# Routed experts on one core: the third tile of rows joins the first weight product, and the last output product moves behind the branches' join

## The chip, the cores and the metric

The kernel runs on one core of a Trainium2 chip. The metric is the device time of one execution in microseconds (us), less being better. Three runs of the kernel before took 781.63, 782.46 and 782.55 us; the median is 782.46.

## The reference

Three layers follow each other: windowed attention with 32 global tokens, a gated channel mixer, and a mixture of eight experts. Only the last one is touched:

```python
logits = einsum('bsd,de->bse', x, w_gate)            # x: 4 x 544 x 512, 8 experts
local_gate = sigmoid(einsum('bsd,de->bse', x, w_local))
for b, s:                                            # 2176 tokens in all
    e = argmax(logits[b, s]) if s == 0 or local_gate[b, s] < 0.5 else prev_e
    h = maximum(x[b, s] @ w1[e], 0)                  # 512 -> 1024
    out[b, s] = softmax(logits[b, s])[e] * (h @ w2[e])   # 1024 -> 512
    prev_e = e
```

So each token goes to one expert. With the inputs of the reference (seed 0) experts 0 to 7 get 242, 127, 267, 483, 495, 321, 218 and 23 tokens: 2, 1, 3, 4, 4, 3, 2 and 1 tiles of 128 rows.

## The kernel before

Everything is computed in fp32 pieces: a value is held as a high part (h) and a rest (l), and each product is three matmuls, `mm3` (lines 21, 23 and 24: high times high, high times rest, rest times high). Experts are numbered from 0 here, as in the code.

The first stage (to about 532 us) does the attention, the mixer and the routing, and already computes expert 0's first tile. The second stage, `Experts.run`, goes through the experts one after the other in an order written by hand. For an expert e:

- `gather` (line 862) fetches its rows from `y` in DRAM by index, one indirect DMA of 128 rows (256 KB) for each tile, issued on POOL; `prep` (lines 869 to 872) transposes half of the features of two tiles (four transposes, one group), and ACT and DVE split them into xh and xl.
- `full` computes two tiles at once. The first product ph = w1 x (96 matmuls with 256 moving columns, weights stationary) is split by ACT (line 883) and DVE (line 884) into hh, hl; then `output` makes two products po = h w2, each of 24 matmuls with 512 moving columns.
- `tail` computes one tile: 24 matmuls of 512 columns with the rows stationary (pht), a relu by ACT into hs (line 912), 8 transposes back (`turn`, lines 898 to 901), and 24 matmuls of 512 columns for po.
- DVE scales po (line 927) and POOL scatters it to the output (line 931).
- The next expert's weights come in eight loads of 512 KB (line 769, SP). `split` (lines 778 and 781) makes h on ACT and l on DVE or POOL. `W` is the list of these splits and `X` the list of the preps of the next expert's rows; `full` and `tail` issue them at fixed places between the matmuls. Five load buffers rotate, so a load is issued when a split has freed its buffer.
- The path is chosen at run time from the number of tiles c: `first` compares c>=2 (line 945), then c==1 (949); `more` compares for the third and the fourth tile (938, 939). Every engine runs these branches. A path that is not taken is jumped over.

```python
with tc.If(c>=2) as two:
    s.full(i,e,0,list(W),[*own,*X])
    s.more(i2,e,1,c)
```

In this stage PE takes the instructions in the order of the code; only when a semaphore or a branch holds them does it stand still.

Of the kernel before, what the change touches and what calls it, by code (L numbers as in the profile page):

```python
# [30 lines left out]
LN=8 ; PL=8  # L31
# [4 lines left out]
NR=4; NP=4  # L36
FX=(3,5,6,7); FW=(2,4,6); NW=(2,3); NST=2
LAT=0.2; DLAT=2.1; SLACK=dict(P=0.15,A=0,D=0,G=0)
# [292 lines left out]
class Mix:  # L331
# [17 lines left out]
    def consts(s,const):  # L349
# [20 lines left out]

        s.up=t([P,E],"up"); nc.gpsimd.memset(s.up,float(P-1)); nc.gpsimd.memset(s.up[:,0:1],-1.0)
        s.last=t([1,1],"last"); nc.vector.memset(s.last,0.0)
# [319 lines left out]
    def finish(s,ps):  # L692

        nc=s.nc; t=s.const
        s.ci=t([P,E],"cint",I32); s.cm=t([P,1],"cmax",I32); cf=t([P,E],"cf")
        nc.vector.tensor_tensor(out=s.ci,in0=ps,in1=s.up,op=ALU.add)
        nc.vector.tensor_scalar(out=s.ci,in0=s.ci,scalar1=7,scalar2=None,op0=ALU.logical_shift_right)
        nc.vector.tensor_copy(cf,s.ci)

        ends=cf[:,0:E:E-1]; nc.vector.tensor_scalar(out=ends,in0=ends,scalar1=3.0,scalar2=None,op0=ALU.add)  # L700
        nc.vector.tensor_reduce(out=s.cm,in_=cf,axis=X,op=ALU.max)
# [49 lines left out]
class Experts:  # L751

    def __init__(s,tc,ident,w1,w2,y,out,slots):
        s.tc=tc; s.nc=tc.nc; s.ident=ident; s.w=(w1,w2); s.y=y; s.out=out
        s.w2done=False; s.slots=slots; s.loaded=0; s.staged=[]; s.K=2

        s.o=[1]+[0]*(E-1); s.m=[1]+[NCH]*(E-2)+[1]
    def slot(s,e,which): return s.slots[((2,0),(1,3))[e%2][which]]
# [89 lines left out]
    def alloc(s):  # L848
        w=s.work

        new=[s.xwork.tile([P,1024],F32,name=f"sw{i}",bufs=1) for i in range(NST)]
        s.x=[[s.xwork.tile([P,4,256],F32R,name=f"x{q}{i}",bufs=1) for q in "hl"] for i in range(3)]
        s.h=[w.tile([P,8,256],F32R,name=f"h{q}",bufs=1) for q in "hl"]
        s.st+=new; s.free+=new
    def row(s,e,k):

        return (k+(e>0))%s.K
# [5 lines left out]
    def prep(s,i,e,k,hf):  # L863

        nc=s.nc; xh,xl=s.x[i]; n=min(2,s.m[e]-2*k); N=n*P
# [7 lines left out]
    def full(s,i,e,k,W,X):  # L873

        nc=s.nc; N=256; w1h,w1l=s.views(e,0); xh,xl=s.x[i]; hh,hl=s.h
        def go(L,n=1):
            for _ in range(n):
                if L: L.pop(0)()
        for f in range(8):
            ph=s.ps.tile([P,512],F32,tag="ph",name="ph",bufs=4)[:,:N]  # L880
            fs=slice(f*P,(f+1)*P)
            for d in range(4): mm3(nc,ph,w1h[:,d,fs],w1l[:,d,fs],xh[:,d],xl[:,d],d==0,d==3)
            nc.scalar.activation(hh[:,f],ph,AF.Relu)  # L883
            nc.vector.scalar_tensor_tensor(out=hl[:,f],in0=ph,scalar=0.0,in1=hh[:,f].bitcast(F32),op0=ALU.max,op1=ALU.subtract)  # L884
            if f in FX: go(X)
            if f in FW: go(W)
        for j in range(2):
            s.output(e,2*k+j,slice(j*P,(j+1)*P),lambda: go(W,NW[j]))
        go(W,8); go(X,8)
    def tail(s,i,e,k,W,X,o=None):  # L890
# [12 lines left out]
        go(W,TW[4])  # L903
        for b in range(2):
            ph=s.ps.tile([P,512],F32,tag="ph",name="pht",bufs=4)
            bs=slice(b*512,(b+1)*512)
            for d in range(4):
                if b and d==2:
                    turn(0,hs[0]); go(W,TW[1])
                mm3(nc,ph,xh[:,d,:P],xl[:,d,:P],w1h[:,d,bs],w1l[:,d,bs],d==0,d==3)  # L910
            hs.append(s.work.tile([P,512],F32,tag="hs",name="hs",bufs=1))
            nc.scalar.activation(hs[b],ph,AF.Relu)
            if b==0: go(W,TW[0])
        def within(f):
            if f==TW[2]: turn(1,hs[1])
            if f in (0,3): go(X)
            if f in TW[3]: go(W)
        s.output(e,2*k,slice(0,P),lambda: (go(X,8),go(W,8)),within,o)
    def output(s,e,c,js,between,within=None,held=None):
        nc=s.nc; w2h,w2l=s.views(e,1); hh,hl=s.h; ch=e*NCH+s.o[e]+c  # L920
        po=s.ps.tile([P,512],F32,tag="po",name="po",bufs=2)
        for f in range(8):
            mm3(nc,po,hh[:,f,js],hl[:,f,js],w2h[:,f],w2l[:,f],f==0,f==7)
            if within: within(f)
        between()
        o=s.work.tile([P,512],F32,tag="osb",name="osb",bufs=2) if held is None else held
        nc.vector.tensor_scalar(out=o,in0=po,scalar1=s.pcol[:,ch:ch+1],scalar2=None,op0=ALU.mult)  # L927
        if held is None: s.scatter(e,c,o)
    def scatter(s,e,c,o):
        ch=e*NCH+s.o[e]+c  # L930
        s.nc.gpsimd.indirect_dma_start(out=s.out,out_offset=IndirectOffsetOnAxis(ap=s.idx[:,ch:ch+1],axis=0),in_=o,in_offset=None,bounds_check=T-1,oob_is_err=False)  # L931
    def more(s,i,e,k,c,d=0):

        tc=s.tc
        if 2*k+2>s.m[e]:
            with tc.If(c>=2*k+1+d): s.tail(i,e,k,[],[])
            return
        with tc.If(c>=2*k+1+d):
            with tc.If(c>=2*k+2+d) as two: s.full(i,e,k,[],[])
            with two.Else(): s.tail(i,e,k,[],[])  # L940
    def first(s,i,i2,e,c,W,own,X):

        tc=s.tc; keep=s.loaded,list(s.staged),list(s.free)
        def again(): s.loaded,s.staged,s.free=keep[0],list(keep[1]),list(keep[2])
        with tc.If(c>=2) as two:
            s.full(i,e,0,list(W),[*own,*X])
            s.more(i2,e,1,c)
        with two.Else():
            with tc.If(c==1) as one: again(); s.tail(i,e,0,list(W),list(X))
            with one.Else():  # L950
                again()
                for g in (*W,*X): g()
    def run(s):
        tc=s.tc; K=s.K

        at=lambda e,k: (e%2,2)[k%2]
        s.gather(0,0)
        _,cs=s.nc.values_load_multi_w_load_instructions(s.counts[0:1,0:E],min_val=0,max_val=NCH); cmax=s.nc.values_load(s.cmax[0:1,0:1],min_val=0,max_val=NCH+3)
        s.cs=cs
# [4 lines left out]
        s.fetch()  # L964
        def own(e): return [lambda hf=hf: s.prep(at(e,1),e,1,hf) for hf in range(2)]
        def others(e):
            if e+1>=E: return []
            def last():
                s.prep(at(e+1,0),e+1,0,1)
                if e+2<E: s.gather(e+2,0)  # L970
            def then():
                if e+2<E: s.gather(e+1,1)
                s.prep(at(e+1,0),e+1,0,0)
            return [then,last]

        s.tail(at(0,0),0,0,[s.whole]*min(8,16-LN),others(0))
        for e in range(1,E-1):
            s.first(at(e,0),at(e,1),e,cs[e],[s.whole]*8,own(e),others(e))
        def weights(e):
            for q in range(8): list(s.split(*s.part(e,q,s.st[q%len(s.st)])))  # L980
        def window(e,k,d):
            i=(0,2)[k%2]
            s.gather(e,k); s.prep(i,e,k,0); s.prep(i,e,k,1)
            s.more(i,e,k,cs[e],d)
        def rest(e,o,load=True):

            d=o-(e==0); keep=s.o[e],s.m[e]
            s.o[e]=o; s.m[e]=NCH-o
            with tc.If(cs[e]>=d+1):
                if load: weights(e)  # L990
                for k in range((s.m[e]+1)//2):
                    with tc.If(cs[e]>=2*k+1+d): window(e,k,d)
            s.o[e],s.m[e]=keep

        s.ol=s.xs[0][:,0]
        def end(): s.tail(at(E-1,0),E-1,0,[],[],s.ol)
        with tc.If(cmax<2*K+1) as usual: end()
        with usual.Else():
            rest(E-1,1,False)
            for e in range(E-1): rest(e,2*K if e else 2)  # L1000
            weights(E-1)
            end()
        s.scatter(E-1,0,s.ol)

# [51 lines left out]
```

## Time and profile before

| | us |
|---|---|
| median of three runs | 782.46 (781.63 to 782.55) |
| the profiled execution, its time | 779.67 |
| its span on the core | 777.9 |
| PE busy in the span | 734.8 |
| stage of the experts in the trace | about 532 to 777.9 |

The profile is one execution. Its span is what the trace covers, and its time is 1.8 us longer. A busy share is an average over both stages; for this change only the second counts. [...] "q" behind an engine's name is its sequencer, which reads branches and fills the engine's queue ahead of execution.

### The profile page before, as it was taken

The numbers are of one execution on the slowest core, as the hardware profiler recorded it, in microseconds if no ns is written. First come the engines' busy times: TensorE is split into PE (matmuls) and PEld (weight loads), VectorE is DVE, ScalarE is ACT, GpSimd is POOL, SyncE is SP. The second block draws the span as 40 slices with busy tenths as digits, with TensorE's granted clock in tenths as the row PEclk, the third lists the DMA queues.
The fourth block names the chain that finished last, engine by engine and source line by source line (L and its number), as shares of the span: only waits on it lengthen the run. The fifth ranks groups of instructions, "written<-read, shape, count | busy, mean of one in ns | idle before, by whom it ended". The sixth has DMA issues, their size and how long they took to land.

```text
span 777.9 us, 14122 instructions
## 1 busy us (share of the span) xinstructions
PE 734.8 (94%) x4782; PEld 621.2 (80%) x4782; DVE 510.5 (66%) x1483; ACT 396.3 (51%) x985; POOL 348.1 (45%) x473
## 2 busy tenths in 40 slices
PE   6889897999999999999999899998799999999996
PEld 3656686888888888888888789776698999989884
DVE  6699978878587694796664865666764643617271
ACT  4788665665374673655653524234662622416151
POOL 6567866742546335545443442013664331614231
PEclk9998798999999999999999899999999999999999
DMA  6584223111211211212000500135886341705320
GB/s 151 146 233 135 78 72 115 45 39 34 66 30 40 63 28 37 66 34 75 20 5 28 190 18 11 55 109 190 302 268 216 127 173 52 256 31 178 127 99 17
DMA packets 93478, 77.04 MB, mean 99 GB/s; under 512 B 70462, under 2 KB 74558, under 8 KB 93378
## 3 DMA queue, kind: packets, MB, share of 16 engines
q1 hardware_dynamic: 89618, 64.27, 27.5%
q0 software_dynamic: 3760, 11.54, 4.3%
q8 instruction: 50, 0.82, 0.4%
q14 instruction: 50, 0.41, 0.2%
HBM read 66.87 MB, written 9.70 MB: 98 GB/s over the span
## 4 chain that ended last, share of the span: by engine, by line
PE 68%; DMA 11%; DVE 7%; issue 7%; ACT 3%; SPq 2%; POOL 1%; POOLq 0%; another core or an unknown queue 0%; ACTq 0%; DVEq 0%
DMA out_dram<-osb,idx 8%; PE av L236 5%; PE psk L21 4%; PE psk L23 4%; PE psv L21 4%; PE psv L23 4%; PE psk L24 4%; PE psv L24 4%; PE ptp L228 3%; PE psr L21 2%; PE po L24 2%; PE po L21 2%; PE psr L24 2%; PE po L23 2%; PE psr L23 2%
## 5 line engine op out<-in xcount | busy, mean ns | idle before, releaser
L222 POOL TENSOR_SCALAR pl<-pl,mx 128x192 f32<-128x192 f32 (+1 forms) x128 | 62.7, 502 | 86.1 <-DVE mx L219 40.6
L21 PE MATMUL psk<-xs,slot0h 128*128 128x256 f32 x256 | 75.1, 299 | 0.8 <-ACT xs L446 0.8
L216 ACT ACTIVATE pl<-pl,mx 128x224 f32<-128x224 f32 (+1 forms) x128 | 58.8, 462 | 32.5 <-DVE mx L213 28.3
L23 PE MATMUL psk<-xs,slot0h 128*128 128x256 f32 x256 | 74.3, 291 | 0.0
L24 PE MATMUL psk<-xs,slot0l 128*128 128x256 f32 x256 | 74.0, 290 | 0.0
L448 POOL TENSOR_TENSOR xs<-xm,xs 128x512 fp32r<-128x512 f32 (+1 forms) x36 | 46.3, 1296 | 40.7 <-ACT xs L446 40.7
L883 ACT ACTIVATE hh<-ph 128x256 fp32r<-128x256 f32 x56 | 21.5, 383 | 84.3 <-PE ph L24 82.5
L441 POOL TENSOR_SCALAR xm<-xT,mut 128x256 f32<-128x256 f32 (+7 forms) x96 | 43.4, 467 | 37.7 <-DVE xT L292 17.9
L862 POOL DMA_INDIRECT xs<-y,idx x26 | 33.0, 1271 | 57.5 <-PE pt L869 33.1
L931 POOL DMA_INDIRECT out_dram<-osb,idx x18 | 22.5, 1252 | 77.2 <-DVE osb L927 59.6
L21 PE MATMUL psv<-slot1h,kh 128*128 128x512 f32 x136 | 55.3, 406 | 0.0
L23 PE MATMUL psv<-slot1l,kh 128*128 128x512 f32 x136 | 54.3, 400 | 0.0
L24 PE MATMUL psv<-slot1h,kl 128*128 128x512 f32 x136 | 54.2, 398 | 0.0
L21 PEld LDWEIGHTS psk<-xs,slot0h 128*128 128x128 f32 x256 | 49.4, 196 | 1.8 <-ACT xs L446 0.9
L23 PEld LDWEIGHTS psk<-xs,slot0h 128*128 128x128 f32 x256 | 49.5, 193 | 1.2
L24 PEld LDWEIGHTS psk<-xs,slot0l 128*128 128x128 f32 x256 | 49.6, 194 | 0.6
L228 PE MATMUL ptp<-ident,pl 128*128 128x128 f32 x256 | 43.5, 290 | 4.6 <-DVE kw L119 1.3
L884 DVE SCALAR_TENSOR_TENSOR hl<-ph,hh 128x256 fp32r<-128x256 f32 x56 | 23.7, 423 | 35.3 <-ACT hh L883 34.9
L236 PE MATMUL av<-ph,v 128*128 128x256 f32 x192 | 44.7, 294 | 2.2 <-DVE xT L292 1.8
L444 DVE SCALAR_TENSOR_TENSOR xm<-xT,mut,xm 128x256 f32<-128x256 f32 (+7 forms) x96 | 42.2, 474 | 3.1 <-POOL xm L441 3.0
L119 DVE TENSOR_TENSOR plo<-ptp,ph 128x512 fp32r<-128x512 f32 x48 | 32.7, 685 | 14.9 <-ACT ph L117 14.6
L228 PEld LDWEIGHTS ptp<-ident,pl 128*128 128x128 f32 x256 | 30.4, 147 | 11.3 <-POOL pl L222 1.9
(732 smaller groups left out, 2456.0 us busy)
## 6 DMA issues: line engine op xcount, KB each, us to landing
st<-in_moe_w_dram SPq DMA_DIRECT2D x42, 512.0 KB
sw<-in_moe_w_dram SPq DMA_DIRECT2D x22, 512.0 KB
y<-r SPq DMA_DIRECT2D x17, 256.0 KB
qn<-in_q_l_dram SPq DMA_DIRECT2D x32, 128.0 KB
kn<-in_k_l_dram SPq DMA_DIRECT2D x32, 128.0 KB
earlyh<-in_moe_w_k_dram SPq DMA_DIRECT2D x8, 512.0 KB
raw<-in_moe_w_v_dram SPq DMA_DIRECT2D x8, 512.0 KB
vn<-in_v_l_dram SPq DMA_DIRECT2D x24, 96.0 KB
```

The lines of the kernel that those rows point to most:

```text
L21: i=nc.tensor.matmul(out,wh,xh,start=first,stop=False)
L23: nc.tensor.matmul(out,wh,xl,start=False,stop=False)
L24: return nc.tensor.matmul(out,wl,xh,start=False,stop=last)
L119: nc.vector.tensor_sub(out[1],x,out[0].bitcast(F32))
L216: nc.scalar.activation(p[:,h,ks],p[:,h,ks],AF.Exp,bias=mx[:,h:h+1],scale=-1.0,accum_out=mx[:,4+h:5+h])
L222: nc.gpsimd.tensor_scalar(out=p[:,h,ks],in0=p[:,h,ks],scalar1=mx[:,6+h:7+h],scalar2=0.0,op0=ALU.mult,op1=ALU.add)
L228: nc.tensor.transpose(pt[:,c,h],p[:,h,c*96:c*96+P],s.ident)
L236: nc.tensor.matmul(o,s.v(u,x,i,c),P_[y][:,c],start=c==m==0,stop=c==1 and m==len(parts)-1)
L441: nc.gpsimd.tensor_scalar(out=x[:,u,o:o+k],in0=s.xT[b][:,c,q:q+k],scalar1=m[:,1,c:c+1],scalar2=0.0,op0=ALU.mult,op1=ALU.add)
L444: nc.vector.scalar_tensor_tensor(out=x[:,u,o:o+k],in0=s.xT[b][:,c,1+q:1+q+k],scalar=m[:,0,c:c+1],in1=x[:,u,o:o+k],op0=ALU.mult,op1=ALU.add)
L448: nc.gpsimd.tensor_sub(xl[:,cs,:n],x[:,:,:n],xh[:,cs,:n].bitcast(F32))
L862: s.nc.gpsimd.indirect_dma_start(out=s.xs[i][:,j,:],out_offset=None,in_=s.y,in_offset=IndirectOffsetOnAxis(ap=s.idx[:,ch:ch+1],axis=0))
```

## The change

The counts that steer the branches are now in units of 32 rows (`up`, `finish`; `tiles(n)=4*n-3` is the first unit of tile n). What else changes:

- Expert 1 is computed as one tile without a branch (`one`), as experts 0 and 7 are; rows above it go to the part for rare cases at the end (`rest`).
- Experts 2 to 6 go through `expert`. A third tile of up to 96 rows is not computed by itself any more: `joined(N)` runs the first product once over N = 288, 320 or 352 rows, then a product for the third tile with 32, 64 or 96 rows stationary (`out_`), then the second tile's product. Which N is chosen stands in a row of comparisons, c>=5, 9, 10, 11, 12, each nested in the one before. From 12 units on `big` runs two tiles and then the third and fourth as before.
- The first tile's output product (for `big` the third's) stands behind the join of all paths (`s.product(0,...)` at the end of `expert`), with the scaling and scatter of bank 1 ahead of it. Which rows it belongs to is copied by POOL into `at` and `by` at the head of each path.
- The third tile's rows are gathered as before and transposed in the expert before (`third`, one group of four transposes, `prep1`); the fourth tile's in `big` alone (`own`).
- Five weight splits stand on each path and three behind the join. x is held for 512 rows in two tiles, h for 352; hs shares the buffers of osb; the descriptor scratch of the indirect DMAs is 4096 bytes instead of 8192.

```diff
-FX=(3,5,6,7); FW=(2,4,6); NW=(2,3); NST=2
+FX=(3,5,7); WJ=(288,320,352); MW=352; FW=(2,4,6); NW=(2,3); NST=2
+def tiles(n): return 4*n-3
-        s.o=[1]+[0]*(E-1); s.m=[1]+[NCH]*(E-2)+[1]
+        s.o=[1]+[0]*(E-1); s.m=[1,1]+[NCH]*(E-3)+[1]
...
+    def wide(s,i,e,N,W=(),X=()):
+        nc=s.nc; W=list(W); X=list(X); w1h,w1l=s.views(e,0); xh,xl=s.rows(i,N); hh,hl=[t[:,:,:N] for t in s.h]
         for f in range(8):
             ph=s.ps.tile([P,512],F32,tag="ph",name="ph",bufs=4)[:,:N]
...
+    def product(s,b,e,js,within={}):
+        w2h,w2l=s.views(e,1); hh,hl=s.h; n=js.stop-js.start
         for f in range(8):
+            mm3(s.nc,s.bank[b][:n],hh[:,f,js],hl[:,f,js],w2h[:,f],w2l[:,f],f==0,f==7)
+            for g in within.get(f,()): g()
+    def place(s,b,pc,idx,n=P,o=None):
+        held=o is not None
+        if not held: o=s.work.tile([P,512],F32,tag="osb",name="osb",bufs=2)[:n]
+        s.nc.vector.tensor_scalar(out=o,in0=s.bank[b][:n],scalar1=pc[:n],scalar2=None,op0=ALU.mult)
+        if not held: s.scatter(o,idx[:n])
...
+    def one(s,i,e,b,W,X,o=None):
+        W=list(W); last=s.tall(i,e,[W.pop(0) for _ in range(min(5,len(W)))])
+        g=dict((f,[]) for f in range(8)); g[TW[2]].append(last)
+        for f,x in zip((0,3,4),X): g[f].insert(0,x)
+        for f,w in zip(TW[3],W): g[f].append(w)
+        s.product(b,e,slice(0,P),g); s.place(b,*s.cols(e,0),o=o)
...
-    def first(s,i,i2,e,c,W,own,X):
+    def expert(s,i,i2,e,c,rows,own,X,third):
+        tc=s.tc; keep=s.loaded,list(s.staged),list(s.free); W=[s.whole]*5
+        def begin(k=0,early=True):
+            s.loaded,s.staged,s.free=keep[0],list(keep[1]),list(keep[2])
+            ch=e*NCH+s.o[e]+2*k
+            s.nc.gpsimd.tensor_copy(s.at,s.idx[:,ch:ch+2]); s.nc.gpsimd.tensor_copy(s.by,s.pcol[:,ch:ch+2])
+            if early: rows()
+        def second(W): s.product(1,e,slice(P,2*P),dict(zip((0,2),([w] for w in W))))
+        def big():
+            begin(1,False)
+            s.wide(i,e,256,W[:3],[own,lambda: (rows(),X[0]()),X[1]])
+            s.out_(0,e,0,slice(0,P),{2:W[:1]}); s.out_(1,e,1,slice(P,2*P),{2:W[:1]})
+            with tc.If(c>=tiles(4)) as four:
+                s.wide(i2,e,256); second([])
+            with four.Else(): s.tall(i2,e,[],[])
+        def joined(N):
+            begin()
+            s.wide(i,e,N,W[:3],X)
+            if N>256: s.out_(0,e,2,slice(256,N))
+            second(W[:2])
...
+        def chain(k):
+            if k==len(L): big(); return
+            with tc.If(c>=tiles(3)+k+1) as up: chain(k+1)
+            with up.Else(): joined(L[k])
+        with tc.If(c>=tiles(2)) as two:
+            with tc.If(c>=tiles(3)) as up: chain(0)
+            with up.Else(): joined(256)
+        with two.Else():
+            with tc.If(c>=1) as some: single()
+            with some.Else(): none()
+        s.place(1,s.by[:,1:2],s.at[:,1:2])
+        s.product(0,e,slice(0,P),{1:[third],2:[s.whole],4:[s.whole],6:[s.whole]})
+        s.place(0,s.by[:,0:1],s.at[:,0:1])
...
-        s.tail(at(0,0),0,0,[s.whole]*min(8,16-LN),others(0))
-        for e in range(1,E-1):
-            s.first(at(e,0),at(e,1),e,cs[e],[s.whole]*8,own(e),others(e))
+        for e in range(2):
+            rows(e); s.one(at(e,0),e,e,[s.whole]*min(8,16-LN if e==0 else 8),[*others(e),lambda: third(e)])
+        for e in range(2,E-1):
+            s.expert(at(e,0),at(e,1),e,cs[e],lambda: rows(e),lambda: own(e),others(e),lambda: third(e))
...
-    nc=_bacc.Bacc("TRN2",target_bir_lowering=False,num_devices=1,dynamic_dma_scratch_size=8192)
+    nc=_bacc.Bacc("TRN2",target_bir_lowering=False,num_devices=1,dynamic_dma_scratch_size=4096)
```

`tall` is `tail` up to its second `turn`; `wide` is the first half of `full`. Three places of PE's order show the moves.

The end of expert 0 and the start of expert 1 on PE, before (slot1 holds expert 1's w1; what follows L945 is the two-tile path, which expert 1 jumps over):

```order
L21 MATMUL po<-slot0h,hh 128x512
L23 MATMUL po<-slot0l,hh 128x512
L24 MATMUL po<-slot0h,hl 128x512
L945 COMPARE_AND_BRANCH
L21 MATMUL ph<-xh_7284,slot1h 128x256
```

and of the change:

```order
L23 MATMUL po_7291<-slot0l,hh 128x512
L24 MATMUL po_7291<-slot0h,hl 128x512
L21 MATMUL po_7291<-slot0h,hh 128x512
L23 MATMUL po_7291<-slot0l,hh 128x512
L24 MATMUL po_7291<-slot0h,hl 128x512
L21 MATMUL pht<-slot1h,xh_7285 128x512
```

The branch is gone, and expert 1's single tile follows directly.

The third tile of expert 2 on PE, before (the second tile's last matmuls, the jump at the end of the two-tile path of lines 938 and 939, the start of the tile by itself):

```order
L23 MATMUL po<-slot3l,hh 128x512
L24 MATMUL po<-slot3h,hl 128x512
L939 UNCONDITIONAL_BRANCH
L21 MATMUL pht<-slot1h,xh_7286 128x512
L23 MATMUL pht<-slot1l,xh_7286 128x512
```

and of the change, on the path for 288 rows (the end of the first product, the start of the third tile's product):

```order
L23 MATMUL ph<-xl_7284,slot2h 128x288
L24 MATMUL ph<-xh_7283,slot2l 128x288
L21 MATMUL ph<-xh_7283,slot2h 128x288
L23 MATMUL ph<-xl_7284,slot2h 128x288
L24 MATMUL ph<-xh_7283,slot2l 128x288
L21 MATMUL po_7291<-slot0h,hh 32x512 [waits Activation_49]
L23 MATMUL po_7291<-slot0l,hh 32x512
L24 MATMUL po_7291<-slot0h,hl 32x512
```

The 24 pht matmuls and the 8 transposes of the third tile are gone; the first product is 32 columns wider, and 24 matmuls with 32 rows stationary follow it.

The join of expert 2's paths on PE in the change (the preps of the empty path, its jump, then the first tile's product and the transposes of expert 3's third tile):

```order
L873 MATMUL pt<-ident,xs_5855 128x128 [waits DVE_49,PE_49]
L873 MATMUL pt<-ident,xs_5855 128x128 x3
L996 UNCONDITIONAL_BRANCH
L21 MATMUL po_7291<-slot0h,hh 128x512 [waits DVE_49,Activation_49]
L23 MATMUL po_7291<-slot0l,hh 128x512
L24 MATMUL po_7291<-slot0h,hl 128x512
L21 MATMUL po_7291<-slot0h,hh 128x512
L23 MATMUL po_7291<-slot0l,hh 128x512
L24 MATMUL po_7291<-slot0h,hl 128x512
```

Before, nothing but the next expert stood behind the join; now 24 matmuls do, whose first one waits for DVE and ACT to have reached the join.

## Rows read from the trace of the kernel before

**Rows 1.** The page: busy us, share of the span and instructions of each engine.
```profile
PE 734.8 (94%) x4782; PEld 621.2 (80%) x4782; DVE 510.5 (66%) x1483; ACT 396.3 (51%) x985; POOL 348.1 (45%) x473
```

**Rows 2.** Stretches of experts 0 to 3, 5, 6: length, busy (matmuls), clock, DMA share, GB/s.
```profile
533.39:548.74 15.35, 13.92 (x64) 1.00 0.87 296
548.74:567.64 18.90, 14.66 (x65) 0.91 0.86 300
567.64:604.07 36.43, 36.40 (x218) 1.00 0.68 232
604.07:650.93 46.86, 46.84 (x306) 1.00 0.38 131
697.71:733.99 36.28, 36.26 (x218) 1.00 0.49 160
733.99:758.90 24.91, 23.91 (x156) 1.00 0.24 83
```

**Rows 3.** Who waited for whom, PE, 530 to 778: total, times, longest.
```profile
PE pht L21 <- DVEq L938: 1.0, 1, 1.0
```

**Rows 4.** Stretches of PE: a 256-wide pass, two 512-wide products, two single tiles.
```profile
628.50:640.01 11.51, 11.51 (x97) 1.00 0.45 175
640.01:650.93 10.92, 10.92 (x50) 1.00 0.07 26
591.84:604.07 12.23, 12.23 (x59) 1.00 0.43 160
721.98:733.99 12.01, 12.01 (x59) 1.00 0.35 134
```

**Rows 5.** The chain in order of time, expert 2: four transposes of one group.
```profile
573.62 0.44 PE pt L869 x4
```

**Rows 6.** Branches on PE's sequencer by line: ns min/median/max, start of the first and last.
```profile
L945 PEldq COMPARE_BRANCH  x1: 7044/7044/7044, 545.7 to 545.7; - x1
L939 PEldq COMPARE_BRANCH  x1: 3896/3896/3896, 587.9 to 587.9; - x1
L939 PEldq COMPARE_BRANCH  x1: 318/318/318, 718.0 to 718.0; - x1
L938 PEldq COMPARE_BRANCH  x1: 3343/3343/3343, 753.7 to 753.7; - x1
```

**Rows 7.** PE in order of time, behind the branches at 545.7 and 587.9: start, length, idle before.
```profile
552.98 0.49 PE L21 MATMUL pht<-slot1h,xh 128*128 128x512 f32 x1 [4.24 <-issue]
591.59 0.39 PE L24 MATMUL po<-slot0h,hl 128*128 128x512 f32 x1
591.84 0.51 PE L21 MATMUL pht<-slot2h,xh 128*128 128x512 f32 x1
```

**Rows 8.** ACT in order of time, expert 1.
```profile
554.90 1.06 ACT L778 ACTIVATE slot2h<-st 128x1024 fp32r<-128x1024 f32 x1 [2.62 <-DMA st<-in_moe_w_dram]
557.68 0.60 ACT L912 ACTIVATE hs<-pht 128x512 f32<-128x512 f32 x1 [1.72 <-PE pht L24]
558.81 0.60 PE L898 MATMUL pht<-ident,hs 128*128 128x128 f32 x4
```

**Rows 9.** Stretches of PE around expert 1: length, busy, clock, DMA share, GB/s.
```profile
545.00:550.00 5.00, 3.74 (x19) 1.00 0.78 254
550.00:555.00 5.00, 2.02 (x6) 0.84 0.96 357
560.00:565.00 5.00, 5.00 (x30) 1.00 0.63 211
553.40:556.70 3.30, 3.30 (x10) 0.50 1.04 377
```

**Rows 10.** PE in order of time, first stage, and the granted clock behind it.
```profile
129.00 0.50 PE L207 MATMUL s__1598<-kw,qT 64*128 64x192 f32 x1 [3.14 <-ACT pg L265]
130.00:133.00 3.00, 3.00 (x8) 0.50 0.00 0
```

**Rows 11.** DMA issues, 545 to 553: count, median us to landing.
```profile
xs<-y,idx POOLq DMA_INDIRECT x4, 8.2
```

More of the change, by code (lines that the diff above doesn't have):

```diff
@@ L872, in prep, with prep1, go @@
         nc.vector.tensor_sub(xl[:,sl,:N],pt[:,:,:N],xh[:,sl,:N].bitcast(F32))
[L873 to L878, printed above, removed]
+    def prep1(s,i,e,k,j):
+        nc=s.nc; js=slice(j*P,(j+1)*P); xh,xl=[t[:,:,js] for t in s.rows(i)]
+        pt=s.ps.tile([P,4,P],F32,tag="pt",name="pt1",bufs=2)
+        for d in range(4): nc.tensor.transpose(pt[:,d],s.xs[s.row(e,k)][:,j,d*P:(d+1)*P],s.ident)
+        nc.scalar.activation(xh,pt,AF.Copy)
+        nc.vector.tensor_sub(xl,pt,xh.bitcast(F32))
+    def go(s,L,n=1):
+        for _ in range(n):
+            if L: L.pop(0)()
+    def wide(s,i,e,N,W=(),X=()):
+        nc=s.nc; W=list(W); X=list(X); w1h,w1l=s.views(e,0); xh,xl=s.rows(i,N); hh,hl=[t[:,:,:N] for t in s.h]
         for f in range(8):
@@ L932, in more, with out_ @@
+    def out_(s,b,e,c,js=slice(0,P),within={}):
+        s.product(b,e,js,within); s.place(b,*s.cols(e,c),n=js.stop-js.start)
+    def one(s,i,e,b,W,X,o=None):
[4 more added lines that the diff above has]
+        s.product(b,e,slice(0,P),g); s.place(b,*s.cols(e,0),o=o)
     def more(s,i,e,k,c,d=0):
@@ L934, in more, with single @@
         tc=s.tc
+        def single():
+            s.tall(i,e,[],[]); s.out_(0,e,2*k)
         if 2*k+2>s.m[e]:
-            with tc.If(c>=2*k+1+d): s.tail(i,e,k,[],[])
+            with tc.If(c>=tiles(2*k+1+d)): single()
             return
-        with tc.If(c>=2*k+1+d):
-            with tc.If(c>=2*k+2+d) as two: s.full(i,e,k,[],[])
-            with two.Else(): s.tail(i,e,k,[],[])
-    def first(s,i,i2,e,c,W,own,X):
[L943 to L947, printed above, removed]
-        with two.Else():
[L949 to L952, printed above, removed]
+        with tc.If(c>=tiles(2*k+1+d)):
+            with tc.If(c>=tiles(2*k+2+d)) as two:
+                s.wide(i,e,256)
+                for j in range(2): s.out_(j,e,2*k+j,slice(j*P,(j+1)*P))
+            with two.Else(): single()
@@ L964, in run, with own, rows, then @@
         s.fetch()
-        def own(e): return [lambda hf=hf: s.prep(at(e,1),e,1,hf) for hf in range(2)]
+        def own(e): s.prep1(at(e,1),e,1,1)
+        def rows(e):
+            if s.m[e+1]>2: s.gather(e+1,1)
         def others(e):
-            if e+1>=E: return []
+            def then(): s.prep(at(e+1,0),e+1,0,0)
             def last():
@@ L988, in rest, with end @@
             s.o[e]=o; s.m[e]=NCH-o
-            with tc.If(cs[e]>=d+1):
+            with tc.If(cs[e]>=tiles(d+1)):
                 if load: weights(e)
                 for k in range((s.m[e]+1)//2):
-                    with tc.If(cs[e]>=2*k+1+d): window(e,k,d)
+                    with tc.If(cs[e]>=tiles(2*k+1+d)): window(e,k,d)
             s.o[e],s.m[e]=keep
         s.ol=s.xs[0][:,0]
-        def end(): s.tail(at(E-1,0),E-1,0,[],[],s.ol)
-        with tc.If(cmax<2*K+1) as usual: end()
+        def end(): s.one(at(E-1,0),E-1,1,[],[],s.ol)
+        with tc.If(cmax<8*K+1) as usual: end()
         with usual.Else():
             rest(E-1,1,False)
-            for e in range(E-1): rest(e,2*K if e else 2)
+            for e in range(E-1): rest(e,(2,1)[e] if e<2 else 2*K)
             weights(E-1)
             end()
-        s.scatter(E-1,0,s.ol)
+        s.scatter(s.ol,s.cols(E-1,0)[1])
 def program(tc,ins,out):
```

82 lines of the change are left out of this document (38 added, 44 removed).

## The prediction

> **What bounds the kernel now.** I read the page first: PE is busy for 94% of the span, the other engines far less [rows 1]. That is an average, so I cut the second stage into its experts [rows 2]. Experts 2, 3, 5 and 6 keep PE busy to within 0.04 us of the whole stretch, except for 1.0 us at the end of expert 6. Expert 1 holds PE for only 14.66 of its 18.90 us, with DMA 86% busy, and expert 0 for 13.92 of 15.35. So from expert 2 on what counts is how long PE's own instructions take, and in experts 0 and 1 what PE waits for. The list of waits names the 1.0 us: expert 7's first matmul waits for DVE's sequencer at the join of line 938 [rows 3]. PE in order of time shows the largest hole, 4.24 us ahead of expert 1, with "issue" as its releaser: no data was late [rows 7]. The row of the branch explains it. PE's sequencer took 7.04 us for the branch of line 945, which began at 545.7 while queued matmuls still ran [rows 6]. Behind the hole the granted clock was 0.50 [rows 9].
>
> **The third tile (experts 2 and 5).** Now it costs a tail of 12.23 us in expert 2 and of 12.01 us in expert 5 [rows 4]. Instead the 96 matmuls of the first product get 32 columns more for expert 2 (267 rows, 9 units, N=288) and 96 more for expert 5 (321 rows, 11 units, N=352), and 24 matmuls of 512 columns are added. A 256-column matmul takes 11.51/96 = 0.120 us and a 512-column one 10.92/48 = 0.2275 us [rows 4], so a column costs 0.00042 us. Widening is 96x32x0.00042 = 1.3 us and 96x96x0.00042 = 3.9 us; the 24 matmuls are 5.5 us (their moving side is the same 512 columns). Balance: -12.2+1.3+5.5 = **-5.5** and -12.0+3.9+5.5 = **-2.7**, together -8.2 us. The trace has no width between 256 and 512. The bounds are a widening that is free (-5.2 us more) and one that costs as much as 512 columns at once (96x0.1076 = 10.3 us for each expert, in place of 1.3 and 3.9). I take the straight line, since 288 lies next to the 256 row and the two rows nearly double with the columns. ACT and DVE work on wider tiles, but they are busy for only 51% and 66% of the span [rows 1], with four ph buffers between.
>
> **Transposes.** A group of four costs 0.44 us [rows 5]. Expert 2 and expert 5 lose one group each, expert 6 two, expert 1 gains one (expert 2's third tile): **-1.3 us**. Experts 3 and 4 have the same four groups and the same products: 0.
>
> **The join ahead of expert 7.** DVE's scaling of expert 6's last product and its branch now run beside 24 matmuls, and expert 7's rows and buffers are long ready: **-1.0 us** [rows 3]. If this cover went, the 1.0 us would be back.
>
> **Expert 1 without a branch.** An undisturbed tile takes 12.01 us [rows 4]; with the two groups that prepare expert 2 it is 12.9. Expert 1 takes 18.90, so 6.0 us are at stake: the 4.24 us hole and some 1.8 us of half clock behind it. But the next stall is near. ACT runs three weight splits ahead of the first relu, and the third waits for its load until 554.90; the relu itself ran at 557.68, when the late matmuls were done, and the transposes on PE at 558.81 [rows 8]. With PE on time ACT is the bound: 554.90+1.06+0.60 lets the transposes start at 556.6, 2.2 us earlier. Three gathers of 256 KB that expert 0 issues for expert 1's further tiles are gone from this stretch, where DMA moves some 300 GB/s [rows 2], 0.79 MB or 2.6 us of its time; the gathers for expert 2 come behind expert 0's scatter instead. Half of that as earlier landing gives 1.3 us. PE then stands still for some 2 us, and the clock may fall again: it was at 0.50 behind holes of 4.24 and of 3.14 us [rows 7, 9, 10]. A quarter of 1.8 us, -0.5. Estimate **-3.0 us**, bounds -0.5 and -6.0. Expert 0's own small savings end in the same wait and count nothing. Expert 2's third rows are now gathered only in expert 1 and needed some 8 us later; gathers landed a median of 8.2 us after issue here [rows 11]. I put **+0.3** for a wait there, bounds 0 and 3.
>
> **New jumps.** A comparison itself is cheap, and five in a row are read while PE's queue is full. A jump is dear when its target must be fetched: lines 939 and 938 took 3.90 and 3.34 us on PE's sequencer, though one at line 939 with the same distance (144 matmuls) took 0.32 [rows 6]. Such a jump is hidden as long as queued matmuls last. The one of 587.9 ended just in time, the next matmul follows at 591.84 without idle time [rows 7]; the one of 753.7 ended ahead of the matmuls at 757.9. So about 4 us are covered behind a dense run of 512-column products, but only 3 us at the end of a single tile: line 945 began at 545.7 and the matmuls ended at 548.7.
>
> The change makes seven long jumps. At the entry expert 2 skips `big` and two wider paths (about 610 matmuls), expert 5 `big` (310), expert 6 `big` and three paths (760). At the join experts 2, 3, 4 and 5 skip 180, 660, 660 and 480 matmuls. Entries of 5 and 6 and all joins lie behind 24 to 48 such products, cover 4 us against 3.3 to 3.9: I put 0.2 us for each, 1.2 us. Expert 2's entry lies behind expert 1's single tile, cover 3 us; DMA was 63% busy there [rows 9], like the 68% of expert 2 [rows 2] where a jump took 3.90 us: 0.9, and 0.5 for contention. Sum **+2.6 us**. Bounds: 0, and for expert 2's entry 7.04-3.0 = 4 us and half clock behind it. [...]
>
> **Rest.** DVE, ACT and POOL jump too, some 1 us or more behind PE; ph buffers cover four feature blocks of 1.5 us each on the entry, 24 matmuls on the join. POOL's two small copies and the earlier gathers delay only rows that are used at the expert's end. The smaller descriptor scratch can hold a gather back by at most what one takes to land, 8.2 us [rows 11]; except in expert 1 (counted) 20 us cover it. All of this: 0.
>
> **Sum.** -8.2-1.3-1.0-3.0+0.3+2.6 = **-10.6 us** on the profiled execution's 779.67 us, so 769.1. The median of the runs is 2.8 us above that execution; I keep this distance: 782.46-10.6 = **771.9 us**.
>
> **Rivals.**
> - *Contended entry* (15%). Expert 2's entry fetches while weights and gathers fill the DMA queues, as line 945 did at a share of 0.96 [rows 9]: 4 us exposed and 1.8 us of half clock in place of 1.4, thus 4.4 more: 776.3. For it: the 7.04 us. Against: the same stretch had 63%.
> - *Nothing but gain* (15%). Loads land early enough for all 6.0 us in expert 1, and the jumps hide but for 0.3: 771.9-3.0-0.3-2.3 = 766.3. For it: the 0.32 us jump.
> - *Slower: jumps that meet an empty queue* (5%). The product behind the join starts with a wait for DVE and ACT and holds transposes with three waits; if these keep PE's queue empty, each of the seven jumps costs its 3.3 to 3.9 us whole, 25 us in place of 2.6, so +11.8: 794. It decides from 1.9 us exposed for each jump, where the other terms (13.2 us) are used up. Against it: the two long jumps behind dense products were hidden. [...]
> - *The shared pass is not taken* (2%). Were a third tile above 96 rows, `big` would compute it by itself and 8.2 us would stay: 780.1. The counts speak against it.
>
> **How the numbers follow.** The forecast has 63%. Its own range, with the line of widths, expert 1 and the entry off by half their bounds, is 768.5 to 775.5. The range that is to hold 8 in 10 reaches to the contended entry and nearly to the case of gain: 766.5 to 777.0. About 0.2%, 1.6 us, is what a measurement of this kernel tells from no change. Faster by more: 0.92; within: 0.03; slower: 0.05.
>
> **What would show it.** Right: no pht of experts 2 and 5 in the profile; 96 matmuls of 128x288 in about 12.8 us and of 128x352 in 15.4; expert 2 in about 30.5 us and expert 5 in 33; expert 1 with no "issue" hole but a wait of ACT on a load; no wait on DVE ahead of expert 7; jumps of 3 to 4 us on PE's sequencer with holes below 1 us. Wrong: holes with "issue" or a DVE sequencer as releaser ahead of each expert or behind each join, a granted clock of 0.50 behind them, or wide matmuls that take more than the line says.

## The result and the profile after

Four runs of the changed kernel took 770.85 to 773.99 us, median 773.36; four runs of the kernel before beside them 780.58 to 782.55, median 782.05. The ratio is 0.9898 with a 95% interval of 0.986 to 0.9936: 8 us faster, more than the 0.2% that a measurement can tell from no change. The forecast was 771.9 us with a range of 766.5 to 777.0.

The profiled execution took 773.22 us, its span is 771.5. Here are the page's line of busy times and then the stretches of PE from expert 0 to expert 7, each from one expert's first matmul to the next one's (length, busy (matmuls), granted clock as a share of full speed, DMA share, GB/s). They answer to [rows 1] and [rows 2].

```profile
PE 726.4 (94%) x4702; PEld 611.4 (79%) x4702; DVE 496.9 (64%) x1477; ACT 389.9 (51%) x974; POOL 345.0 (45%) x480
```

```profile
536.77:549.89 13.12, 12.84 (x61) 1.00 0.90 317
549.89:566.31 16.42, 14.04 (x69) 1.00 0.91 327
566.31:601.34 35.03, 32.26 (x181) 0.95 0.54 185
601.34:648.41 47.07, 47.07 (x305) 1.00 0.41 135
648.41:695.74 47.33, 46.98 (x306) 1.00 0.42 137
695.74:730.77 35.03, 33.62 (x181) 1.00 0.59 172
730.77:753.85 23.08, 23.08 (x149) 1.00 0.40 141
753.85:765.97 12.12, 12.12 (x57) 1.00 0.08 27
```

The hole ahead of an expert's first matmul stands in the row of the expert before it, but for expert 2, whose row begins with its hole. Experts 0 and 1 together went from 34.25 to 29.54 us (-4.7), expert 2 from 36.43 to 35.03 (-1.4), experts 3 and 4 together from 93.64 to 94.40, expert 5 went from 36.28 to 35.03 (-1.25) and expert 6 from 24.91 to 23.08 (-1.8). From expert 0's first matmul to PE's last it is 237.64 before and 229.20 after: **-8.4 us**. The stretches of before in [rows 2] are cut where an expert's last matmul ends, up to 0.17 us behind the next one's first; nothing below hangs on that. Two rows of before are needed for these sums, that of expert 4 and PE's last matmul, which ends at 771.04:

```profile
650.93:697.71 46.78, 46.78 (x306) 1.00 0.38 135
...
770.65 0.39 PE L24 MATMUL po<-slot3h,hl 128*128 128x512 f32 x1
```

Expert 0 begins 3.4 us later, at 536.77 instead of 533.39, and the time behind PE's last matmul is 5.5 us instead of 6.9; the last of the experiments comes back to both.

The list of waits of PE, 530 to 771 us, says what stands in those stretches:

```profile
PE ph L21 <- issue: 4.5, 3, 2.8
PE pht L904 <- ACT slot2h L779: 1.8, 1, 1.8
PE pht L904 <- ACT hs L918: 0.5, 1, 0.5
```

The join's wait of [rows 3] is gone. New is a wait with "issue" as releaser (a hole, below: PE stands still though no data is late), three times ahead of a wide pass: 2.77, 0.35 and 1.41 us at the entries of experts 2, 5 and 6. PE in order of time around the first and the last of them:

```profile
565.91 0.40 PE L24 MATMUL po<-slot3h,hl 128*128 128x512 f32 x1
569.08 0.58 PE L21 MATMUL ph<-xh,slot2h 128*128 128x288 f32 x1 [2.77 <-issue]
...
728.97 0.40 PE L24 MATMUL po<-slot3h,hl 128*128 128x512 f32 x1
730.77 0.39 PE L21 MATMUL ph<-xh,slot2h 128*128 128x256 f32 x1 [1.41 <-issue]
```

Behind the first hole the granted clock was 0.50, and the DMA share had been 0.99 ahead of it and 0.93 ahead of the last one (stretches of all engines: length, busy of PE, PEld, DVE, ACT, POOL, then clock, DMA share, GB/s):

```profile
569.10:572.10 3.00, 3.00 (x13) 3.00 (x14) 0.00 (x0) 0.00 (x0) 2.66 (x5) 0.50 0.86 284
...
562.00:569.00 7.00, 4.31 (x23) 3.23 (x21) 5.00 (x6) 4.02 (x5) 4.54 (x3) 0.99 0.99 365
724.00:731.00 7.00, 5.59 (x28) 4.26 (x27) 4.00 (x5) 3.44 (x4) 3.28 (x2) 1.00 0.93 262
```

The twelve matmuls up to 572.10 took 3.02 us; at the 0.133 us that one of 288 columns takes at full clock they are 1.6, so the half clock cost 1.4 us. The holes and it make 2.77+0.35+1.41+1.4 = **5.9 us**.

The branches on PE's sequencer (ns min/median/max, start of the first and last) are what [rows 6] was before. Line 990 is the row of comparisons in `chain`, line 993 the comparison c>=9, line 974 the one for the fourth tile in `big`; the last record of a line at the end of a path is the jump to the join.

```profile
L990 PEldq COMPARE_BRANCH  x1: 5790/5790/5790, 563.1 to 563.1; - x1
L990 PEldq COMPARE_BRANCH  x1: 3700/3700/3700, 591.2 to 591.2; - x1
L974 PEldq COMPARE_BRANCH  x1: 3532/3532/3532, 638.2 to 638.2; - x1
L974 PEldq COMPARE_BRANCH  x1: 3393/3393/3393, 685.1 to 685.1; - x1
L990 PEldq COMPARE_BRANCH  x2: 64/1988/3913, 691.5 to 691.7; - x2
L990 PEldq COMPARE_BRANCH  x1: 3679/3679/3679, 719.0 to 719.0; - x1
L993 PEldq COMPARE_BRANCH  x1: 5532/5532/5532, 725.2 to 725.2; - x1
```

These are the seven long jumps that the prediction counted. (An eighth, at the program's end, is in both kernels: 3.46 us on line 997 before, 3.45 us on line 1047 here.) The four at the joins took 3.4 to 3.7 us and left no hole. The three at the entries are the three holes, and two of them took 5.5 and 5.8 us. A comparison in the row of `chain` that falls through takes 64 ns.

Two moments of each jump can be read beside these rows: the trace's records of DMA packets have one 16 KB packet of the queue "q8 instruction" inside each of the seven, and PE's last queued matmul ends some time after the jump's start. Five of them, in us:

| jump | until its packet starts | packet | until the sequencer goes on | in all | PE still had work for |
|---|---|---|---|---|---|
| entry of 2, 563.1 | 3.37 | 1.05 | 1.37 | 5.79 | 3.18 |
| join of 2, 591.2 | 0.87 | 1.41 | 1.42 | 3.70 | all of it |
| join of 4, 685.1 | 0.89 | 1.03 | 1.47 | 3.39 | all of it |
| entry of 5, 691.7 | 1.33 | 1.18 | 1.40 | 3.91 | 3.73 |
| entry of 6, 725.2 | 2.96 | 0.89 | 1.68 | 5.53 | 4.18 |

The last two columns give the holes: 5.79-3.18 = 2.6, 3.91-3.73 = 0.2, 5.53-4.18 = 1.35, each 0.06 to 0.2 us below the measured hole. What differs most between these five is the time until the packet starts, 0.87 to 3.37 us. In the kernel before the long jumps of [rows 6] (7.04, 3.90 and 3.34 us) hold one such packet each too, and the jump of 0.32 us at 718.0 holds none. That led to **theory A**: a jump waits for its target's code, whose packet stands behind weight loads and gathers when these fill the DMA engines. **Rival B**: a jump is the longer, the more code it skips (the entry of expert 6 skips some 760 matmuls, that of expert 5 only 310). By the prediction's counts it stands badly already: the joins of experts 3 and 4 skip 660 matmuls and took 3.5 and 3.4 us. **Rival C**: the holes are no fetch at all but a wait for data or for another engine at the branch.

### The profile page after: what moved, and what is told of

Read it like the earlier page. It is cut to its first block, busy times and chain, and to the rows that moved or that the text cites. A ratio compares the mean times of both kernels' runs of the same rounds, so it can differ in the third digit from the quotient of the medians.

```text
span 771.5 us, 13972 instructions
## 1 busy us (share of the span) xinstructions
PE 726.4 (94%) x4702; PEld 611.4 (79%) x4702; DVE 496.9 (64%) x1477; ACT 389.9 (51%) x974; POOL 345.0 (45%) x480
## 5 line engine op out<-in xcount | busy, mean ns | idle before, releaser
L894 ACT ACTIVATE hh<-ph 128x256 fp32r<-128x256 f32 (+2 forms) x56 | 22.4, 400 | 76.3 <-PE ph L24 45.9
L895 DVE SCALAR_TENSOR_TENSOR hl<-ph,hh 128x256 fp32r<-128x256 f32 (+2 forms) x56 | 24.7, 442 | 44.2 <-ACT hh L894 42.2
L866 POOL DMA_INDIRECT xs<-y,idx x23 | 24.8, 1078 | 46.9 <-PE pt L873 22.4
L21 PE MATMUL ph<-xh,slot2h 128*128 128x256 f32 (+1 forms) x128 | 37.9, 296 | 4.2 <-issue 4.2
```

Of the source, the lines that this page charges most:

```text
L21: i=nc.tensor.matmul(out,wh,xh,start=first,stop=False)
L866: s.nc.gpsimd.indirect_dma_start(out=s.xs[i][:,j,:],out_offset=None,in_=s.y,in_offset=IndirectOffsetOnAxis(ap=s.idx[:,ch:ch+1],axis=0))
```

## The experiments

The first stage's end moves by several us from one execution to the next, so beside the ratio each experiment is read in its own second stage: from expert 0's first matmul to PE's last, 229.20 us for the change. Two pairs of executions show how far this length moves: 237.64 and 237.27 us for the kernel before, 229.20 and 230.15 for the change, the second of each pair with a smaller descriptor scratch.

**The taken path first.** In experts 2, 5 and 6 the comparisons are turned so that the path these inputs take stands first in the code; all paths remain.

```diff
+        if near==256:
+            with tc.If(c<tiles(3)) as up:
+                with tc.If(c>=tiles(2)) as two: joined(256)
+                with two.Else(): low()
+            with up.Else(): chain(0)
...
+                        with tc.If(c==tiles(3)+k) as at: joined(near)
+                        with at.Else(): others(0)
...
+            s.expert(at(e,0),at(e,1),e,cs[e],...,near={2:288,5:352,6:256}.get(e))
```

> Edit: in experts 2, 5 and 6 the path that is taken stands first in the code, so no engine jumps at the entry; all arithmetic is the same. Theory A (code fetch): the three holes at the entries of the changed kernel (2.77 us with about 1.3 us of half clock behind it, 0.35 and 1.40 us) are jumps whose target code comes late; all three vanish, 5.8 us in all, so 773.4-5.8 = 767.6 us, ratio to before 0.982. The joins keep their jumps of 3.4 to 3.7 us on PE's sequencer, behind 24 dense products, with holes below 0.4 us. Rival C (the holes are a wait on data or on another engine at the branch): they stay, 773.4 us, ratio 0.990. Rival B (a jump's length grows with the code that it skips): also 767.6, it is told apart by the lengths of the joins' jumps.

Measured: 766.86 us median (764.38 to 769.24), ratio 0.98 with an interval of 0.9772 to 0.9828, which lies wholly below the change's. The second stage is 223.88 us, 5.3 shorter. PE's waits from 541 us on, and the stretches of experts 1, 2, 5 and 6:

```profile
PE po L21 <- ACT hh L906: 1.1, 1, 1.1
PE po L21 <- DVE osb L932: 0.9, 1, 0.9
PE pht L904 <- ACT hs L918: 0.7, 1, 0.7
```

```profile
549.21:565.63 16.42, 14.53 (x70) 10.62 (x68) 13.33 (x13) 10.75 (x15) 12.29 (x8) 1.00 0.91 321
565.63:596.41 30.78, 30.78 (x181) 25.75 (x180) 15.49 (x21) 13.25 (x20) 13.57 (x12) 1.00 0.63 214
690.29:723.72 33.43, 33.43 (x182) 29.56 (x180) 15.23 (x20) 13.02 (x19) 12.74 (x11) 1.00 0.55 171
723.72:747.80 24.08, 23.20 (x149) 20.76 (x148) 13.84 (x18) 11.31 (x18) 10.62 (x7) 1.00 0.47 152
```

No "issue" is left, and experts 2 and 5 keep PE busy for the whole of their stretches. So the holes were the jumps, and C falls. The other joins' jumps took 3.3 to 3.8 us without a hole, near the 3.4 to 3.7 expected. But one wait came in a new place: expert 6's path now ends with a long jump to the join (line 997), where before it had a short one, and this jump was longer (its code packet started only after 2.30 us; the DMA share was 0.56 from 737 to 740 us):

```profile
L997 PEldq COMPARE_BRANCH  x1: 4690/4690/4690, 737.3 to 737.3; - x1
```

It took 4.69 us against 3.98 us of queued work. The 0.88 us that PE then stood still are put down to DVE in the list of waits, because the first matmul behind the join waits on it too; the place and the jump's end at 741.99 (that matmul starts at 742.16) show the jump. Expected were holes below 0.4 us at the joins.

**The loads taken away.** What remains between A and B is why 5.8 and 5.5 us.

```diff
-        (queue or s.nc.sync).dma_start(...)
+        if e<3: (queue or s.nc.sync).dma_start(...)
```

> Edit: the change without the weight loads of experts 3 to 7 (they compute with what the buffers last held); the splits, gathers, scatters, branches and all matmuls stay. Theory A (code fetch behind queued loads): a jump is 0.9 to 1.0 us until its 16 KB move, 1.0 to 1.4 us for them and 1.4 us until the sequencer runs on; the 5.79 us ahead of expert 2 and the 5.53 us ahead of expert 6 were longer only because the fetch waited 3.4 and 3.0 us behind weight loads. Without them both take 3.3 to 4.0 us, the hole ahead of expert 6 is 0 to 0.2 us and that ahead of expert 2 at most 1.0 us; the stage from expert 0's first matmul to the end is 3 to 5 us shorter than the change's 234.7 us. Rival B (a jump's length grows with the code that it skips): 5.5 to 5.8 us stay at both places and both holes stay.

Measured: one execution took 764.42 us. The branches at the entries of experts 2 and 6, and the list of PE's waits from 541 us on:

```profile
L990 PEldq COMPARE_BRANCH  x1: 3930/3930/3930, 559.5 to 559.5; - x1
L993 PEldq COMPARE_BRANCH  x1: 3815/3815/3815, 718.0 to 718.0; - x1
```

```profile
PE ph L21 <- issue: 1.5, 1, 1.5
PE po L21 <- ACT hh L906: 0.9, 1, 0.9
```

Both jumps fell to 3.8 and 3.9 us with the same code skipped, so B falls as well: what shrank is the time until the packet starts (3.37 us became 1.57, 2.96 became 0.92), and the weight loads had made it long. The hole ahead of expert 6 is gone. The one ahead of expert 2 stays at 1.5 us, where at most 1.0 was expected: behind expert 1's single tile PE's queue held only 2.6 us of work. The second stage is 224.98 us, 4.2 shorter, within the 3 to 5 expected.

**The first tile's product back inside the paths.**

```diff
+        def close():
+            s.place(1,s.by[:,1:2],s.at[:,1:2])
+            s.product(0,e,slice(0,P),{1:[third],2:[s.whole],4:[s.whole],6:[s.whole]})
+            s.place(0,s.by[:,0:1],s.at[:,0:1])
...
-            second(W[:2])
+            second(W[:2]); close()
```

> Edit: the first tile's product stands at the end of each path again instead of behind the join, everything else as in the change. Theory A (code fetch): the jump to the join is then followed at once by the next expert's entry jump, with the same 4 us of queued products to cover both: holes of about 3.3 us ahead of expert 5 (3.4+3.9-4) and 3.7 to 5.2 us ahead of expert 6 in place of 0.35 and 1.40, some half clock behind each, and the wait of 1.0 us ahead of expert 7 is back. Together +5 to +10: 778 to 783 us. Rival (the move is worth only the 1.0 us of the last join, as the prediction counted it): 774.4 us.

Measured: 788.95 us median (786.69 to 792.99), ratio 1.0091 (1.0058 to 1.0124): slower than the kernel before, and worse than expected. The second stage is 246.45 us, 17.2 longer than the change's. PE's waits, and the two branches that follow each other at the end of expert 5 (line 996 ends the path, line 999 is the entry of expert 6):

```profile
PE ph L21 <- issue: 16.6, 4, 7.1
```

```profile
L996 PEldq COMPARE_BRANCH  x1: 4643/4643/4643, 736.6 to 736.6; - x1
L999 PEldq COMPARE_BRANCH  x1: 6303/6303/6303, 741.5 to 741.5; - x1
```

PE's last queued matmul ended at 740.93, before the first jump was over; the second one lies bare, 7.07 us. It is longer too, and the trace has two code packets in it. Behind every jump of the change a further packet starts 0.7 to 1.6 us after its end, so one of the two may belong to the first jump; which code they carry isn't in the trace. Ahead of expert 5 the pair leaves 5.94 us. The expectation let the cover be used up by the sum of two jumps, but took the shorter lengths. So the 24 matmuls behind the join are worth some 16 us (medians) to 17 us (second stage) here, not 1: they are what hides the jump to the join and fills the queue again before the next entry. One part of the expectation did not come: PE doesn't wait ahead of expert 7 (no DVE in its waits), so the wait of [rows 3] stays away without this product too.

**Expert 1 through the branches again.**

```diff
-        s.m=[1,1]+[NCH]*(E-3)+[1]
+        s.m=[1]+[NCH]*(E-2)+[1]
...
-        for e in range(2):
+        for e in range(1):
...
-        for e in range(2,E-1):
+        for e in range(1,E-1):
```

> Edit: expert 1 goes through the same branches as experts 2 to 6, everything else as in the change. Theory A (code fetch): PE's jump at its entry stands behind a single tile while weight loads keep DMA busy, takes 5.5 to 7 us like the ones of 5.8 and 7.0 seen under such load, and leaves a hole of 2.8 to 4.2 us and 1.3 to 1.8 us of half clock behind it; the 1.84 us that expert 1 now waits for ACT's split of a late load are inside it. Net +2 to +4: 775.4 to 777.4 us, ratio 0.992 to 0.994. Rival (expert 1 is bound by its loads anyway, a branch costs nothing): 773.4 us within 0.5. Rival B (length by distance, 360 skipped matmuls took 7.0 us, about 740 would take 14): 782 or more.

Measured: 777.81 us median (773.71 to 779.87), ratio 0.9926 (0.9897 to 0.9954). The second stage is 233.72 us, 4.5 longer. The jump was not the long one that was expected; its row, and the first of PE's waits:

```profile
L992 PEldq COMPARE_BRANCH  x1: 3900/3900/3900, 551.7 to 551.7; - x1
```

```profile
PE pht L904 <- ACT hs L918: 3.9, 2, 3.6
PE po L23 <- issue: 1.5, 1, 1.5
PE ph L21 <- issue: 1.2, 1, 1.2
PE pht L21 <- issue: 1.2, 1, 1.2
```

It left a hole of only 1.2 us. The larger part is a wait for ACT's relu of 3.6 us, where the change has 1.8: ACT stands still for loads, first until 556.39, then until 560.38, and the relu behind its splits runs at 563.13 only. Experts 0 and 1 together take 36.97 us up to the end of expert 1's last matmul, 7.4 more than in the change, and 2.3 of them lie in expert 0 (15.45 against 13.12). In return expert 2's entry, the change's worst, took 3.98 us against 4.03 of queued work and left 0.1 us instead of a hole of 2.8 and 1.4 of half clock. So the size came near to the expected (+4.4 us in the median) partly by luck, and the mechanism came half: the branch costs a hole, and expert 1 waits longer for loads. That its further gathers delay these is argued, not shown. The 1.5 us of "issue" stand in the middle of expert 3's product behind the join, 649.19 to 650.68. The jump to the join had ended at 647.50; a second code packet started at 648.15 and took 1.11 us, and with the 1.4 us of the table that gives 650.66. That PE stood still for this packet is read from its times alone; no run tried it.

**The third tile by itself.**

```diff
-WJ=(288,320,352)
+WJ=()
```

> Edit: no joined pass; the third tile of experts 2 and 5 is computed by itself again, everything else as in the change. Theory (the third tile is worth the sum in the prediction): its 8.2 us come back and two groups of transposes, 0.9 us; in return experts 2 and 5 take the first path in the code and lose the holes at their entries (4.1 and 0.35 us): 773.4+9.1-4.4 = 778.1 us, ratio 0.995. Without the jumps' share it would be 782.5. Rival (the joined pass itself brings little, its wider tiles wait for ACT and DVE): 769 to 773 us.

Measured: 775.77 us median (774.13 to 779.88), ratio 0.9908 (0.9877 to 0.9938), which overlaps with the change's: by the time alone the joined pass can't be told from none. The second stage can: 234.07 us, 4.9 longer than the change's (4.7 expected), 10.2 longer than with the taken path first, where no entry has a hole either. The stretches of experts 2 and 5 against 30.78 and 33.43 there:

```profile
568.23:605.76 37.53, 36.84 (x218) 31.80 (x216) 17.89 (x25) 16.03 (x25) 15.06 (x13) 1.00 0.54 176
699.66:737.25 37.59, 36.81 (x217) 31.89 (x216) 17.08 (x24) 15.43 (x24) 14.15 (x12) 1.00 0.51 155
```

That is 6.75 and 4.16 us, 10.9 in all: the 8.2 of the prediction, 0.9 for two groups of transposes, and twice 0.69 us in which the single tile's transposes wait for ACT's relu, which leaves 0.4. The joined pass gains what it was said to; the change gives half of it back at the entries.

**ACT's order in expert 1.** On top of the first experiment, ACT runs two splits ahead of expert 1's first relu instead of three.

```diff
-        W=list(W); last=s.tall(i,e,[W.pop(0) for _ in range(min(5,len(W)))])
+        W=list(W); last=s.tall(i,e,[W.pop(0) for _ in range(min(4 if e==1 else 5,len(W)))],lead=2 if e==1 else TW[4])
...
+        if e==1: g[0].append(W.pop(0))
```

> Edit: the version with the taken paths first, and in expert 1 ACT runs two weight splits ahead of its first relu instead of three, the later ones one place later each. Theory (PE's waits of 1.07 and 0.74 us in expert 1 are relus queued on ACT behind splits that wait for loads): both nearly vanish, -1.0 to -1.8 us: 765.1 to 765.9 us against 766.9, ratio 0.978. Rival (expert 1 is bound by the loads themselves): the waits return at the next expert or at expert 1's output product, 766.9 us within 0.7.

Measured: 766.26 us median (763.27 to 767.33), ratio 0.9799 (0.9765 to 0.9833), not to be told from 0.98. The second stage is 223.48 us, 0.4 shorter than the first experiment's. PE's waits:

```profile
PE po L24 <- DVE hl L907: 1.9, 2, 1.3
PE po L21 <- ACT slot3h L779: 0.7, 1, 0.7
```

Expert 1's waits moved on by one step: its relus are no longer late, but the rest of h, `hl` on DVE, now is (0.68 and 1.26 us). The second line is not expert 1's: it stands at 740.58 to 741.27, at expert 6's join, where the long jump of the first experiment took 4.51 us this time. The rival's sign came, the waits returned at expert 1's output product. Its reason, the loads, is not shown: from 549.72 to the first late `hl` at 555.48 DVE works on weight splits without a pause, and ACT waits for loads only 0.76 and 0.38 us in that expert.

**The descriptor scratch.** Two runs for the end of the program, with `dynamic_dma_scratch_size=2048` in the change and 4096 in the kernel before.

> Edit: the change with 2048 bytes of descriptor scratch instead of 4096. From PE's last matmul to the end of the span were 6.9 us with 8192 bytes (before) and 5.3 to 5.8 us with 4096 (the change and its variants), POOL's drain at the end being 5.1 and 3.6 us. Theory (the scratch's size sets that drain): 4.6 to 5.2 us now. Rival (it is the scatter's landing or the code at the end): 5.3 to 5.8 us. Cost side: if gathers are held back for lack of descriptors, a PE wait on gathered rows appears in experts 1 to 3.

> Edit: the kernel before with 4096 bytes of descriptor scratch instead of 8192, nothing else. Theory (the scratch's size sets the end): 5.3 to 5.8 us from PE's last matmul to the end of the span instead of 6.9. Rival (the change's other edits shortened the end): 6.9 us. Also a second look at the first stage, which took 3.4 us longer in the changed kernel's profiled execution: if that is the run and not the change, expert 0's first matmul is not at 533.4 us again here but anywhere between 533 and 539.

From PE's last matmul to the end it was 6.35 us with 2048, outside both expectations, and 5.55 us in the kernel before with 4096; the seven other versions with 4096 lie between 5.27 and 5.85. So a smaller scratch does not simply shorten the end. With 8192 and 2048 bytes there is one profile each, so whether the size has a part in the 1.4 us between 6.9 and 5.5 stays open. No wait on gathered rows appeared with 2048, so that a smaller scratch holds gathers back, as the prediction allowed for, is not shown. Expert 0's first matmul was at 535.38 in this run of the kernel before and at 531.30 in that of the change, against 533.39 and 536.77 in the first ones; over all versions of the change it lies between 531.30 and 539.14. So the 3.4 us by which the first stage was longer are within what executions of one kernel differ by, and are not read as an effect of the change.

## Why the prediction was right

The time lay within the range and 1.5 us from the forecast, but two terms were off in opposite directions, so that it lay so close is partly luck. In the second stage of the profiled executions, by the prediction's own steps:

| step | predicted | measured |
|---|---|---|
| third tile, transposes and join, experts 2 to 6 | -10.5 | -9.7 |
| experts 0 and 1, third gather | -2.7 | -4.7 |
| new jumps | +2.6 | +5.9 |
| sum | -10.6 | -8.4 |

The second executions (with the smaller scratch) say how firm this is: experts 0 and 1 took 34.25 and 33.0 us before, 29.54 and 30.0 after, so their gain is 3.0 to 4.7 us, and the sum -7.1 to -8.4.

- **Third tile: right.** A matmul of 288 columns takes 0.133 us, 96 of them 12.8 us, and one of 352 columns 0.160 us, 96 of them 15.4, both as said; the 24 with 32 rows stationary take 5.5 us (584.26 to 589.78). Without its hole and its half clock expert 2 takes 30.8 us (said: 30.5), and expert 5 without the hole behind it 33.6 (said: 33). The straight line from 256 to 512 columns holds at these two widths.
- **Transposes and join: right in size, the reason for the join's 1.0 us not shown.** Expert 6 lost 1.83 us where 1.9 was said, and nothing waits ahead of expert 7. But nothing waits there either with the product back inside the paths. In the kernel before the comparison of line 938 stands behind expert 6's products, in the change all comparisons of that path stand ahead of them; that this took the wait away fits, but no run tried it. Not foreseen are 0.4 us that experts 3 and 4 take longer together.
- **Expert 1 without a branch: right in kind, the sum with expert 0 too small.** The hole became a wait of ACT for a load, as said; [rows 8] has the split behind its load at 554.90, here it is this one:

```profile
554.38 1.06 ACT L779 ACTIVATE slot2h<-st 128x1024 fp32r<-128x1024 f32 x1 [2.68 <-DMA st<-in_moe_w_dram]
555.34 0.58 ACT L918 ACTIVATE hs<-pht 128x512 f32<-128x512 f32 x1
```

  Expert 1 itself gained 2.5 us against the 3.0 said. The failed step is "Expert 0's own small savings end in the same wait and count nothing": expert 0 became 2.2 us shorter (1.2 between the second executions; fewer transposes, and no wait at its output product, which was 1.02 and 0.42 us before), and expert 1 did not wait longer for it. It hangs on the branch: with expert 1 branched again expert 0 takes 15.45 us (15.35 in the kernel before). No wait for the third rows was seen (0.3 said).
- **New jumps: right in kind, 3.3 us too small.** Two steps failed. For expert 2's entry "DMA was 63% busy there" was read from the kernel before, and from 560 to 565 us, ahead of the time in which the jump would have run (564.5 to 567.6 has 0.85 there). In the change the share was 0.99 from 562 to 569, and the contended rival came true in most of its size: 2.77 us of hole and 1.4 of half clock, 4.2 in all, where 1.4 was put and the rival had 5.8. That expert 1's being shorter brought the entry nearer to the loads fits the branched version, where this jump took 3.98 us; nothing tried it by itself. For expert 6's entry "cover 4 us against 3.3 to 3.9" had the cover right (4.18) and the jump wrong (5.53): the length was taken from two jumps without asking what DMA did meanwhile. The joins came out at 0, where 0.8 was put.
- The contended entry thus happened inside the forecast; that the total still came out close is owed to experts 0 and 1. Neither the third tile left by itself nor a jump on an empty queue came about. With the product back inside the paths two jumps do begin on an empty queue (holes of 5.9 and 7.1 us); the rival counted seven, so that its 794 us lie near to that kernel's 789 is chance.

Each of the seven long jumps holds a 16 KB packet of the instruction queue. Together they took 29.5 us; 4.5 of these were paid as holes, and the queued matmuls covered the other 25.0. The 1.4 us of half clock came on top.

## What to carry to other kernels

In this kernel a long jump cost time only where the queue ahead of it held less work than the jump took: 3.4 to 3.9 us at DMA shares of 0.02 to 0.32 and 5.5 and 5.8 us at 0.93 and 0.99 (in the kernel before 7.0 at 0.83, but also 3.9 at 0.85), against 3.2 to 4.2 us of queued matmuls at the entries. So let the likely path stand first in the code, put a dense run of work behind each join so that two jumps never follow each other, and look at what loads are in flight at a jump in the changed order of work, not in the old one. And when the first stage moves by several us between executions, compare the stage that was changed: the median could not tell the joined pass from none, the second stage could: 4.9 us, where two executions of nearly the same kernel differ by 0.4 and by 1.0.

## What was not expected of the hardware

- The fetch of code was held up by weight loads: the same two jumps took 5.79 and 5.53 us beside weight loads and 3.93 and 3.82 without them. Once its packet had started, a jump took another 2.4 to 2.8 us in all seven cases. The kernel before shows such a spread with the same code: in its execution with the smaller scratch the jump of 587.9 took 4.68 us instead of 3.90, and 0.64 us of it lay bare.
- Two jumps in a row: with the product inside the paths the entries of experts 5 and 6 took 5.77 and 6.30 us, with two code packets inside each. With expert 1 branched PE stood still for 1.49 us behind a join until just after a further packet; that this packet stopped it is read from the times alone.
- A hole of 2.8 us ahead of expert 2 was followed by 3 us of granted clock 0.50, one of 1.4 us ahead of expert 6 was not, nor a wait of 1.8 us in expert 1 (1.00 behind both). With the product inside the paths the two slices of 20 us that hold the holes of 5.9 and 7.1 us have a mean granted clock of 0.8 and 0.7 in the page. The slices with the hole of 0.9 us (the taken path first) and of 1.5 us (expert 1 branched) have 0.9 or more there, and so have those behind them.
